# Token layers of a fused attention and mixer kernel: one pair of heads at a time, or two pairs in matmuls of 256 columns

## The chip, the cores and the metric

The kernel runs on one core of a Trainium2 chip. The metric is the device time of one execution in microseconds (us); lower is better. TensorE (PE in the profile) multiplies matrices into PSUM, VectorE (DVE) and ScalarE (ACT) read PSUM and write SBUF, GpSimd (POOL) works on SBUF, and SyncE (SP) issues most of the DMAs.

## The reference

```python
def reference(q, k, v, tau, w_tok1, w_tok2, w_ch1, w_ch2):   # q, k, v: (8, 12, 448, 64)
    q_n = q / (norm(q, axis=-1) + 1e-6)
    k_n = k / (norm(k, axis=-1) + 1e-6)
    attn = softmax(q_n @ k_n.transpose(0, 1, 3, 2) / tau)
    x = (attn @ v).transpose(0, 2, 1, 3).reshape(8, 448, 768)
    xt = x.transpose(0, 2, 1)
    h = relu(xt @ w_tok1) @ w_tok2          # token layers: 448 -> 256 -> 448
    u = x + h.transpose(0, 2, 1)
    return u + relu(u @ w_ch1) @ w_ch2      # channel layers: 768 -> 1536 -> 768
```

All inputs and the output are float32; the matmuls run in fp16 with float32 sums.

## The kernel before

The work is cut into 48 pairs of heads, six for each of the eight batches. A pair gives 128 of the 768 channels, so a pair's attention output `x` is 448 tokens by 128 channels, held as a tile of four windows of 128 tokens (tile `x`, 128 partitions, 4 x 128). The main loop has one turn for each pair from 7 to 47; here such a turn is called a segment and has its pair's number. An instruction stream is written out by hand in the order of the program, and each engine works its instructions in that order.

A segment `i` issues, in this order:

- three `score` calls for pair `i` (L345): matmuls of 64 rows into tiles `psS`, each followed by an exponential on ScalarE (L346);
- the value product of pair `i - 1`: `pv_rest` (L367, eight matmuls that alternate between the two tiles `psO_0` and `psO_1`) and `pv` (L384, 24 matmuls), then on VectorE a reciprocal (L387) and the scaling that writes `x` (L388). For the pairs below 12 there is no `pv_rest`, and the 32 matmuls of `pv` fill `psO_0` first and `psO_1` after it;
- `side(i)`: casts, squares and norms of later pairs on GpSimd and VectorE, loads and DMA transposes of later pairs on SP (`tpose_dma`, L330);
- one `unit(True)`, a piece of the channel layers of an earlier batch: `m_ch1` (tile `psG`, six matmuls of 448 columns, L467, and a ReLU on ScalarE, L470) or `m_ch2` (tile `psF`, twelve matmuls of up to 384 columns, L483, and one or two additions on VectorE, L487);
- `score_rest` (tile `psQ`, L352);
- `tok2(i - 2)`: the second token layer, eight matmuls of 128 columns into `psU` (L434), then the addition of `x` on VectorE (L437), which writes `u16`, then `udma`: a DMA transpose into `ut` on SP (L443). The channel layers read `ut`;
- below segment 13, `tpose(i + 1)`: transposes on TensorE into a tile `pst` (L322) and a copy on VectorE (L324);
- as many further units as are due by a budget in nanoseconds (`fed`, `due`): the first of them as `unit(True)`, all others as `unit()`;
- `tok1(i - 1)`: the first token layer, eight matmuls of 128 columns into `psR` (L420), then a ReLU on VectorE (L423) that writes `rt`;
- `sums(i + 3)`: a reduction on VectorE (L266).

PSUM has two pools, and a tile is given the slot that comes next in turn. What the order of the work means for a slot is that the first matmul of a tile waits until the reader of the slot's last tile has ended:

```python
    ps = ctx.enter_context(tc.tile_pool(name="ps", bufs=2, space=bass.MemoryType.PSUM))
    ps2 = ctx.enter_context(tc.tile_pool(name="ps2", bufs=3, space=bass.MemoryType.PSUM))
```

`psO_0`, `psO_1`, `psU`, `psR`, `pst` and the units called as `unit()` (here: narrow units) take the two slots of `ps` (tag `b`) in turn. `psS`, `psQ` and the units called as `unit(True)` (wide units) take the three slots of `ps2`.

After segment 47 a tail computes the channel layers of the last two batches with fewer products (`p1` to `p7`, L587; `q1` to `q7`, L675).

Of the kernel before, what the change touches and what calls it, by code (L numbers as in the profile page):

```python
# [7 lines left out]
FP32 = mybir.dt.float32  # L8
FP16 = mybir.dt.float16
AF = mybir.ActivationFunctionType  # L10
ALU = mybir.AluOpType
# [5 lines left out]
def _bcast_free(ap: bass.AP, n: int) -> bass.AP:  # L17
    new_ap = list(ap.ap) + [[0, n]]
    return bass.AP(tensor=ap.tensor, offset=ap.offset, ap=new_ap)
# [3 lines left out]
def kernel(  # L23
# [12 lines left out]
    nc = tc.nc  # L36

    B, H, S, E = q.shape
# [7 lines left out]
    TT = T // 128  # L46
    DH = 384
    NPAIR = H // 2
    NP_ALL = B * NPAIR
# [20 lines left out]
    def windows(b):  # L70
        return EVEN if b % 2 == 0 else ODD
# [11 lines left out]
    nrm = ctx.enter_context(tc.tile_pool(name="nrm", bufs=3))  # L83
# [6 lines left out]
    ps = ctx.enter_context(tc.tile_pool(name="ps", bufs=2, space=bass.MemoryType.PSUM))  # L90
    ps2 = ctx.enter_context(tc.tile_pool(name="ps2", bufs=3, space=bass.MemoryType.PSUM))

    half = {}
    pipe = {}
    ut = {}
    u16 = {}
    gts = {}

    def old(i):
        return i < OLD  # L100
# [58 lines left out]
    w1t = cst.tile([128, 5, T], FP16, name="w1t")  # L159
    w2n = outp.tile([128, TT, S], FP16, name="w2n", tag="ost")  # L160
    w2t = cst.tile([128, TT, S + 64], FP16, name="w2t")
# [192 lines left out]

    def pv_rest(i):
        if old(i):
            return
        st = pipe[i]  # L360
        st["x"] = nrm.tile([128, 4, 128], FP16, name=f"x_{i}", tag="x", bufs=3)
        st["psO"] = [ps.tile([128, 4, E + 2], FP32, name=f"psO_{i}_{hh}", tag="b") for hh in range(2)]
        for m, lo in enumerate(windows(i // NPAIR)):
            for hh in range(2):
                hb = slice(hh * 64, hh * 64 + 64)
                at = 2 * S * KC + lo
                nc.tensor.matmul(st["psO"][hh][:, m, 0:E + 1], pts[i % 2][hb, at:at + 128],  # L367
                                 vts[(i // HP) % NV][hb, i % HP, 2 * KC, 0:E + 1], start=(m == 0), stop=False)

    def pv(i, hh):  # L370
        st = pipe[i]
        vt = vts[(i // HP) % NV]
        if old(i):
            if hh == 0:
                st["x"] = nrm.tile([128, 4, 128], FP16, name=f"x_{i}", tag="x", bufs=3)
            n, nch = SC, NCH
            psO = ps.tile([128, 4, E + 2], FP32, name=f"psO_{i}_{hh}", tag="b")
        else:
            n, nch = 128, KC
            psO = st["psO"][hh]  # L380
        for m, lo in enumerate(windows(i // NPAIR)):
            for c in range(nch):
                at = (2 * c + hh) * S + lo
                nc.tensor.matmul(psO[:, m, 0:E + 1], pts[i % 2][0:n, at:at + 128], vt[0:n, i % HP, nch * hh + c, 0:E + 1],  # L384
                                 start=(old(i) and c == 0), stop=(c == nch - 1 and (old(i) or m == 3)))
        rec = nrm.tile([128, 4], FP32, name=f"rec_{i}_{hh}", tag="rec", bufs=4)
        nc.vector.reciprocal(out=rec[:], in_=psO[:, :, E])  # L387
        nc.vector.tensor_tensor(out=st["x"][:, :, hh * E:(hh + 1) * E], in0=psO[:, :, 0:E],  # L388
                                in1=_bcast_free(rec[:], E), op=ALU.mult)


    def pv_wide(i):
        st = pipe[i]
        vt = vts[(i // HP) % NV]
        st["x"] = nrm.tile([128, 4, 128], FP16, name=f"x_{i}", tag="x", bufs=3)
        psO = ps2.tile([128, 2, 512], FP32, name=f"psO_{i}", tag="s")
        o = psO[:, :, 0:4 * (E + 2)].rearrange("p h (m e) -> p h m e", m=4)
        for hh in range(2):
            for m, lo in enumerate(windows(i // NPAIR)):
                for c in range(NCH):  # L400
                    at = (2 * c + hh) * S + lo
                    nc.tensor.matmul(o[:, hh, m, 0:E + 1], pts[i % 2][0:SC, at:at + 128],
                                     vt[0:SC, i % HP, NCH * hh + c, 0:E + 1], start=(c == 0), stop=(c == NCH - 1))
        st["o"] = o

    def x_wide(i):
        st = pipe[i]
        o = st["o"]
        rec = nrm.tile([128, 2, 4], FP32, name=f"rec_{i}", tag="rec2", bufs=2)
        nc.vector.reciprocal(out=rec[:], in_=o[:, :, :, E])  # L410
        nc.vector.tensor_tensor(out=st["x"][:].rearrange("p m (h e) -> p h m e", h=2), in0=o[:, :, :, 0:E],
                                in1=_bcast_free(rec[:], E), op=ALU.mult)

    def tok1(i, wide=False):
        st = pipe[i]
        w1 = (0, 1, 2, 3) if (i // NPAIR) % 2 == 0 else (4, 0, 1, 2)
        psR = (ps2 if wide else ps).tile([128, TT, 128], FP32, name=f"psR_{i}", tag="s" if wide else "b")
        for tt in range(TT):
            for m in range(4):
                nc.tensor.matmul(psR[:, tt], w1t[:, w1[m], tt * 128:(tt + 1) * 128], st["x"][:, m],  # L420
                                 start=(m == 0), stop=(m == 3))
        st["rt"] = nrm.tile([128, TT, 128], FP16, name=f"rt_{i}", tag="rt", bufs=2)
        nc.vector.tensor_scalar_max(out=st["rt"][:], in0=psR[:], scalar1=0.0)  # L423

    def tok2(i, pe=False, wide=False):
        st = pipe[i]
        b, pj = i // NPAIR, i % NPAIR
        if pj == 0:
            u16[b] = mix.tile([128, DT, 4, 128], FP16, name=f"u16_{b}", tag="u16", bufs=4)
            ut[b] = mix.tile([128, DT, 4, 128], FP16, name=f"ut_{b}", tag="ut")  # L430
        psU = (ps2 if wide else ps).tile([128, 4, 128], FP32, name=f"psU_{i}", tag="s" if wide else "b")
        for m, lo in enumerate(windows(b)):
            for tt in range(TT):
                nc.tensor.matmul(psU[:, m], w2t[:, tt, lo:lo + 128], st["rt"][:, tt],  # L434
                                 start=(tt == 0), stop=(tt == TT - 1))
        u = u16[b][:, pj]
        nc.vector.tensor_tensor(out=u, in0=psU[:], in1=st["x"][:], op=ALU.add)  # L437
        if not pe:
            udma(i)

    def udma(i):
        b, pj = i // NPAIR, i % NPAIR
        nc.sync.dma_start_transpose(out=ut[b][:, pj], in_=u16[b][:, pj].rearrange("p m d -> p (m d)"))  # L443
# [132 lines left out]
    e = {}  # L576
# [195 lines left out]
    with tc.manual_schedule():  # L772
# [3 lines left out]
            name=nc.get_next_instruction_name(), act_func_set_id=ACT_SET_LN_EXP,  # L776
# [94 lines left out]
        i = NPAIR  # L871
# [48 lines left out]
        for i in range(NPAIR + 1, NP_ALL):  # L920
            b, pj = i // NPAIR, i % NPAIR
            for c in range(KC):
                score(i, c)
                if c == 1 and NP_ALL - 6 <= i < NP_ALL - 2:
                    norms(i + 2)
            if i == NPAIR + 1:
                upose(i - 4, 2)
                tok2(i - 2, pe=True)
                pv_wide(i - 1)
                upose_act(i - 2)  # L930
                x_wide(i - 1)
                sums(i + 2)
            else:
                pv_rest(i - 1)
                pv(i - 1, 0)
                pv(i - 1, 1)
            if i == NP_ALL - 1:
                fast_weights1(2, nc.vector)
            if i == NPAIR + 1:
                refill(0)  # L940
            elif pj == 2 and 1 < b < B - 1:
                refill(b - 1)
            side(i)
            if i == NP_ALL - NPAIR:
                fed[1] = (sum(t for t, _ in queue) - fed[0]) / NPAIR
            fed[0] += fed[1]
            unit(True)
            if old(i):
                score(i, KC)
            else:  # L950
                score_rest(i)
            if i > NPAIR + 1:
                tok2(i - 2)
            if i + 1 < DMA_T0:
                tpose(i + 1)
            if due():
                unit(True)
            while due():
                unit()
            tok1(i - 1)  # L960
            if i + 3 < NP_ALL:
                sums(i + 3)
            if i == NP_ALL - 3:
                early.close()
                tail = ctx.enter_context(tc.tile_pool(name="tail", bufs=1, side="right", reuse_waits="tile"))
                tail_tiles()
            if i == NP_ALL - 2:
                fast_weights2(2, (1,))
                fast_weights1(1, nc.gpsimd)
            if i == NP_ALL - 1:  # L970
                fast_weights1(4, nc.gpsimd)
# [139 lines left out]
```

## Time and profile before

| | us |
|---|---|
| median of 3 runs | 383.1 (382.84 to 383.28) |
| the profiled execution | 380.6 |
| its span, from the first to the last instruction | 378.8 |
| TensorE busy | 366.2 |
| GpSimd, VectorE, ScalarE busy | 286.9, 246.0, 234.0 |
| `psR` matmuls (L420) busy | 29.3 |
| `psU` matmuls (L434) busy | 29.3 |

The profile is that of one execution, 2.5 us below the median of the runs. A matmul's record lasts longer than the time in which the next one can follow it, because matmuls are pipelined: the distance from one start to the next is read off the timeline, where `x8` stands for eight records merged into one line. Segment 13 begins at 79.02 us, segment 47 at 316.93 us, and a segment between them lasts from 4.7 to 8.4 us, according to the units that it holds.

### The profile page before, as it was taken

The numbers are of one execution on the slowest core, as the hardware profiler recorded it, in microseconds if no ns is written. First come the engines' busy times: TensorE is split into PE (matmuls) and PEld (weight loads), VectorE is DVE, ScalarE is ACT, GpSimd is POOL, SyncE is SP. The second block draws the span as 40 slices with busy tenths as digits, with TensorE's granted clock in tenths as the row PEclk, the third lists the DMA queues.
The fourth block names the chain that finished last, engine by engine and source line by source line (L and its number), as shares of the span: only waits on it lengthen the run. The fifth ranks groups of instructions, "written<-read, shape, count | busy, mean of one in ns | idle before, by whom it ended". The sixth has DMA issues, their size and how long they took to land.

```text
span 378.8 us, 10270 instructions
## 1 busy us (share of the span) xinstructions
PE 366.2 (97%) x4086; PEld 240.1 (63%) x4086; DVE 246.0 (65%) x559; ACT 234.0 (62%) x401; POOL 286.9 (76%) x414
## 2 busy tenths in 40 slices
PE   7788999999999999999999999999999999999994
PEld 6466666676567666667656666666666667655562
DVE  7789766777436574557444675456545776887963
ACT  5999887855666447855675466764677574426410
POOL 8999997979667577678657757767869987389760
PEclk9999999999999999999999999999999999999999
DMA  8999999989997898969895798977984874200144
GB/s 225 281 231 218 262 239 200 207 159 157 217 220 141 180 201 209 187 167 170 213 210 121 175 184 198 195 162 197 205 192 104 158 160 99 57 0 3 55 123 116
DMA packets 116256, 64.35 MB, mean 170 GB/s; under 512 B 72304, under 2 KB 112880, under 8 KB 116208
## 3 DMA queue, kind: packets, MB, share of 16 engines
q1 hardware_dynamic: 110208, 58.20, 69.9%
q0 software_dynamic: 5616, 5.21, 8.7%
q8 instruction: 32, 0.52, 0.6%
q10 hardware_dynamic: 384, 0.29, 0.2%
q14 instruction: 16, 0.13, 0.1%
HBM read 43.45 MB, written 11.01 MB: 144 GB/s over the span
## 4 chain that ended last, share of the span: by engine, by line
PE 81%; DMA 7%; DVE 4%; POOL 3%; ACT 1%; issue 1%; SPq 0%; DVEq 0%; POOLq 0%
PE psG L467 21%; PE psF L483 19%; PE psO L384 9%; PE psS L345 7%; PE psU L434 5%; PE psR L420 5%; DMA qf<-in_q_dram 3%; PE psY L587 3%; PE psYo L675 2%; DMA kf<-in_k_dram 2%; PE psX L587 2%; PE psQ L352 2%; POOL kq L298 2%; PE psZ L587 2%; PE psZo L675 1%; DVE ssq L266 1%
## 5 line engine op out<-in xcount | busy, mean ns | idle before, releaser
L346 ACT ACTIVATE pt<-psS 128x896 f16<-128x896 f32 (+1 forms) x156 | 132.7, 916 | 51.9 <-PE psS L345 51.9
L483 PE MATMUL psF<-wc2t,gt 128*128 128x384 f16 x504 | 88.4, 326 | 0.0
L467 PE MATMUL psG<-ut,wc1t 128*128 128x448 f16 x432 | 88.1, 352 | 0.0
L298 POOL TENSOR_TENSOR kq<-kf,rn 128x384 f16<-128x384 f32 (+1 forms) x47 | 41.9, 891 | 59.2 <-DVE rn L275 55.6
L483 PEld LDWEIGHTS <-gt 128*128 128x128 f16 x504 | 47.1, 98 | 27.8
L467 PEld LDWEIGHTS <-wc1t 128*128 128x128 f16 x432 | 40.2, 98 | 32.4
L470 ACT ACTIVATE gt<-psG 128x448 f16<-128x448 f32 x72 | 38.9, 540 | 33.1 <-PE psG L467 33.1
L266 DVE TENSOR_REDUCE ssq<-sq 128x15 f32<-128x960 f32 (+2 forms) x51 | 56.2, 1101 | 2.9 <-ACT sq L248 1.8
L423 DVE TENSOR_SCALAR rt<-psR 128x256 f16<-128x256 f32 x48 | 20.1, 418 | 50.8 <-PE psR L420 50.8
L298 POOL TENSOR_TENSOR kq<-qf,rn 112x512 f16<-112x512 f32 x45 | 47.0, 1045 | 3.0
L345 PE MATMUL psS<-qk 64*128 64x448 f16 x312 | 41.3, 355 | 3.5 <-DVE qk L324 2.8
L487 DVE TENSOR_TENSOR ost<-psF,u 128x384 f32<-128x384 f32 (+1 forms) x48 | 25.7, 536 | 26.8 <-PE psF L483 25.4
L250 POOL TENSOR_TENSOR sq<-qf 112x512 f32<-112x512 f32 x39 | 40.6, 1040 | 0.0
L250 POOL TENSOR_TENSOR sq<-kf 128x384 f32<-128x384 f32 (+1 forms) x46 | 40.2, 873 | 0.3 <-DMA kf<-in_k_dram 0.3
L384 PE MATMUL psO<-vt,pt 128*128 128x65 f16 (+1 forms) x1024 | 39.2, 193 | 0.0
L388 DVE TENSOR_TENSOR x<-psO,rec 128x256 f16<-128x256 f32 x82 | 34.8, 425 | 2.8
L384 PEld LDWEIGHTS <-pt 128*128 128x128 f16 (+1 forms) x1024 | 34.2, 97 | 3.5 <-issue 0.9
L437 DVE TENSOR_TENSOR u<-psU,x 128x512 f16<-128x512 f32 x48 | 32.3, 674 | 2.0 <-PE psU L434 0.5
L434 PEld LDWEIGHTS <-w2t 128*128 128x128 f16 x384 | 24.8, 98 | 7.9 <-issue 1.0
L420 PEld LDWEIGHTS <-w1t 128*128 128x128 f16 x384 | 24.8, 98 | 7.9 <-issue 2.1
L434 PE MATMUL psU<-rt,w2t 128*128 128x128 f16 x384 | 29.3, 219 | 0.5 <-POOL w2t L198 0.5
L420 PE MATMUL psR<-x,w1t 128*128 128x128 f16 x384 | 29.3, 219 | 0.2 <-DVE u L437 0.2
(128 smaller groups left out, 481.0 us busy)
## 6 DMA issues: line engine op xcount, KB each, us to landing
qf<-in_q_dram SPq DMA_DIRECT2D x47, 224.0 KB, 4.2
kf<-in_k_dram SPq DMA_DIRECT2D x36, 192.0 KB, 3.9
vf<-in_v_dram SPq DMA_DIRECT2D x36, 192.0 KB, 3.8
vf<-in_v_dram SPq DMA_DIRECT2D x12, 224.0 KB, 7.6
kf<-in_k_dram SPq DMA_DIRECT2D x11, 224.0 KB, 7.2
wc1t<-in_moe_w_ch_dram POOLq DMA_DIRECT2D x4, 576.0 KB, 10.1
wc2t<-in_moe_w_ch_dram POOLq DMA_DIRECT2D x2, 1152.0 KB, 11.8
out_dram<-ost SPq DMA_DIRECT2D x6, 336.0 KB, 3.6
```

The source lines that it names most:

```text
L250: nc.gpsimd.tensor_mul(out=dst, in0=src, in1=src)
L266: nc.vector.tensor_reduce(out=st["ssq"][0:n, sl], in_=st["sq"][0:n, sl], axis=AXX.X, op=ALU.add)
L298: eng.tensor_tensor(out=kq[0:p, a, 0:n].rearrange("p c g e -> p g c e"), in0=st["kq"[a]][:].rearrange("p (g c) e -> p g c e", g=2), in1=_b ...
L345: nc.tensor.matmul(psS[:, hh, 0:S], qk[hb, c * n:c * n + 128], qm[hb], start=True, stop=True)
L346: nc.scalar.activation(out=pts[i % 2][0:n, 2 * S * c:2 * S * (c + 1)].rearrange("p (h s) -> p h s", h=2), in_=psS[0:n, :, 0:S], func=AF.Ex ...
L384: nc.tensor.matmul(psO[:, m, 0:E + 1], pts[i % 2][0:n, at:at + 128], vt[0:n, i % HP, nch * hh + c, 0:E + 1], start=(old(i) and c == 0), st ...
L388: nc.vector.tensor_tensor(out=st["x"][:, :, hh * E:(hh + 1) * E], in0=psO[:, :, 0:E], in1=_bcast_free(rec[:], E), op=ALU.mult)
L420: nc.tensor.matmul(psR[:, tt], w1t[:, w1[m], tt * 128:(tt + 1) * 128], st["x"][:, m], start=(m == 0), stop=(m == 3))
L434: nc.tensor.matmul(psU[:, m], w2t[:, tt, lo:lo + 128], st["rt"][:, tt], start=(tt == 0), stop=(tt == TT - 1))
L467: nc.tensor.matmul(psG[:, 0:S], wc1t[:, dt, ct * 128:(ct + 1) * 128], ut[b][:, dt].rearrange("p m s -> p (m s)")[:, lo:lo + S], start=(dt ...
L470: nc.scalar.activation(out=gt[:, ct, (b % 2) * S:(b % 2 + 1) * S], in_=psG[:, 0:S], func=AF.Relu)
L483: nc.tensor.matmul(psF[:, 0:hi - lo], gt[:, ct, at:at + 128], wc2t[:, ct, lo:hi], start=(ct == 0), stop=(ct == CT - 1))
```

## The change

From the second batch on, the token layers of two neighbouring pairs (an even one and the odd one after it) are computed together. A tile `xx` holds the `x` of both pairs, and `x_tile(i)` gives a pair its half of it. `tok1(i - 2, 2)` runs in even segments only and computes the first token layer of the pairs `i - 2` and `i - 1` with eight matmuls of 256 columns into one tile `psR`, followed by one ReLU of 512 elements in each partition. `tok2(i - 3, 2)` runs in odd segments only and computes the second layer of the pairs `i - 3` and `i - 2` in two tiles `psU`, each with four matmuls of 256 columns and one addition of 512 elements, and then issues the two DMA transposes. The weights are loaded once for both pairs. The first batch and the last two pairs, 46 and 47, stay one by one. `rt` has one buffer in place of two, of twice the size; `xx` has two in place of the three of `x`.

```diff
+    def x_tile(i):
+        if i % 2 == 0:
+            pipe[i]["xx"] = nrm.tile([128, 4, 2, 128], FP16, name=f"x_{i}", tag="x", bufs=2)
+        pipe[i]["x"] = pipe[i - i % 2]["xx"][:, :, i % 2]
+
     def pv_rest(i):
...
-        st["x"] = nrm.tile([128, 4, 128], FP16, name=f"x_{i}", tag="x", bufs=3)
+        x_tile(i)
...
-    def tok1(i, wide=False):
-        st = pipe[i]
+    def tok1(i, n=1):
         w1 = (0, 1, 2, 3) if (i // NPAIR) % 2 == 0 else (4, 0, 1, 2)
-        psR = (ps2 if wide else ps).tile([128, TT, 128], FP32, name=f"psR_{i}", tag="s" if wide else "b")
+        j = slice(i % 2, i % 2 + n)
+        psR = ps.tile([128, TT, n, 128], FP32, name=f"psR_{i}", tag="b")
         for tt in range(TT):
             for m in range(4):
-                nc.tensor.matmul(psR[:, tt], w1t[:, w1[m], tt * 128:(tt + 1) * 128], st["x"][:, m],
+                nc.tensor.matmul(psR[:, tt], w1t[:, w1[m], tt * 128:(tt + 1) * 128], pipe[i - i % 2]["xx"][:, m, j],
                                  start=(m == 0), stop=(m == 3))
-        st["rt"] = nrm.tile([128, TT, 128], FP16, name=f"rt_{i}", tag="rt", bufs=2)
-        nc.vector.tensor_scalar_max(out=st["rt"][:], in0=psR[:], scalar1=0.0)
-
-    def tok2(i, pe=False, wide=False):
-        st = pipe[i]
+        pipe[i]["rt"] = rt = nrm.tile([128, TT, n, 128], FP16, name=f"rt_{i}", tag="rt", bufs=1)
+        nc.vector.tensor_scalar_max(out=rt[:], in0=psR[:], scalar1=0.0)
+
+    def tok2(i, n=1, pe=False):
         b, pj = i // NPAIR, i % NPAIR
...
-        psU = (ps2 if wide else ps).tile([128, 4, 128], FP32, name=f"psU_{i}", tag="s" if wide else "b")
-        for m, lo in enumerate(windows(b)):
-            for tt in range(TT):
-                nc.tensor.matmul(psU[:, m], w2t[:, tt, lo:lo + 128], st["rt"][:, tt],
-                                 start=(tt == 0), stop=(tt == TT - 1))
-        u = u16[b][:, pj]
-        nc.vector.tensor_tensor(out=u, in0=psU[:], in1=st["x"][:], op=ALU.add)
+        x, rt = pipe[i - i % 2]["xx"], pipe[i]["rt"]
+        for k in range(n):
+            at = range(4 // n * k, 4 // n * (k + 1))
+            psU = ps.tile([128, 4 // n, n, 128], FP32, name=f"psU_{i}_{k}", tag="b")
+            for m in at:
+                lo = windows(b)[m]
+                for tt in range(TT):
+                    nc.tensor.matmul(psU[:, m - at[0]], w2t[:, tt, lo:lo + 128], rt[:, tt],
+                                     start=(tt == 0), stop=(tt == TT - 1))
+            nc.vector.tensor_tensor(out=u16[b][:, pj:pj + n, at[0]:at[-1] + 1].rearrange("p j m d -> p m j d"),
+                                    in0=psU[:], in1=x[:, at[0]:at[-1] + 1, i % 2:i % 2 + n], op=ALU.add)
         if not pe:
-            udma(i)
+            for j in range(n):
+                udma(i + j)
...
-            if i > NPAIR + 1:
-                tok2(i - 2)
+            if i > NPAIR + 1 and i % 2:
+                tok2(i - 3, 2)
...
-            tok1(i - 1)
+            if i % 2 == 0:
+                tok1(i - 2, 2)
+            elif i == NP_ALL - 1:
+                tok1(i - 1)
```

More of the change, by code (lines that the diff above doesn't have):

```diff
@@ L374, in pv @@
             if hh == 0:
-                st["x"] = nrm.tile([128, 4, 128], FP16, name=f"x_{i}", tag="x", bufs=3)
+                x_tile(i)
             n, nch = SC, NCH
@@ L394, in pv_wide @@
         vt = vts[(i // HP) % NV]
-        st["x"] = nrm.tile([128, 4, 128], FP16, name=f"x_{i}", tag="x", bufs=3)
+        x_tile(i)
         psO = ps2.tile([128, 2, 512], FP32, name=f"psO_{i}", tag="s")
@@ L410, in x_wide @@
         nc.vector.reciprocal(out=rec[:], in_=o[:, :, :, E])
-        nc.vector.tensor_tensor(out=st["x"][:].rearrange("p m (h e) -> p h m e", h=2), in0=o[:, :, :, 0:E],
+        nc.vector.tensor_tensor(out=st["x"].rearrange("p m (h e) -> p h m e", h=2), in0=o[:, :, :, 0:E],
                                 in1=_bcast_free(rec[:], E), op=ALU.mult)
-    def tok1(i, wide=False):
-        st = pipe[i]
+    def tok1(i, n=1):
         w1 = (0, 1, 2, 3) if (i // NPAIR) % 2 == 0 else (4, 0, 1, 2)
-        psR = (ps2 if wide else ps).tile([128, TT, 128], FP32, name=f"psR_{i}", tag="s" if wide else "b")
+        j = slice(i % 2, i % 2 + n)
+        psR = ps.tile([128, TT, n, 128], FP32, name=f"psR_{i}", tag="b")
         for tt in range(TT):
             for m in range(4):
-                nc.tensor.matmul(psR[:, tt], w1t[:, w1[m], tt * 128:(tt + 1) * 128], st["x"][:, m],
+                nc.tensor.matmul(psR[:, tt], w1t[:, w1[m], tt * 128:(tt + 1) * 128], pipe[i - i % 2]["xx"][:, m, j],
                                  start=(m == 0), stop=(m == 3))
-        st["rt"] = nrm.tile([128, TT, 128], FP16, name=f"rt_{i}", tag="rt", bufs=2)
-        nc.vector.tensor_scalar_max(out=st["rt"][:], in0=psR[:], scalar1=0.0)
-    def tok2(i, pe=False, wide=False):
-        st = pipe[i]
+        pipe[i]["rt"] = rt = nrm.tile([128, TT, n, 128], FP16, name=f"rt_{i}", tag="rt", bufs=1)
+        nc.vector.tensor_scalar_max(out=rt[:], in0=psR[:], scalar1=0.0)
+    def tok2(i, n=1, pe=False):
         b, pj = i // NPAIR, i % NPAIR
```

## The prediction

> **What bounds the kernel.** I read the page first (busy shares, chain of waits, groups), then busy time by stretch, then the timeline of TensorE and VectorE around the token layers.
>
> ```profile
> PE 366.2 (97%) x4086; PEld 240.1 (63%) x4086; DVE 246.0 (65%) x559; ACT 234.0 (62%) x401; POOL 286.9 (76%) x414
> PE 81%; DMA 7%; DVE 4%; POOL 3%; ACT 1%; issue 1%; SPq 0%; DVEq 0%; POOLq 0%
> ```
>
> ```profile
> 79.00:289.00 210.00, 210.00 (x2341) 137.29 (x2339) 120.30 (x298) 130.81 (x234) 150.49 (x245) 1.00 0.85 183
> ```
>
> TensorE has no gap from 79 to 289 us (210.00 of 210.00, full clock), and the chain is its matmuls. There every nanosecond given to or taken from TensorE's stream counts; other engines count only where TensorE waits for them. From 289 to 310 us the chain passes through POOL and a DMA transpose, but segment 46's first score waits only some 0.25 us for it.
>
> Next, the end of segment 23, with a narrow `psG` before `psR`:
>
> ```profile
> 157.12 0.61 PE L420 MATMUL psR<-x,w1t 128*128 128x128 f16 x8
> 157.32 0.54 ACT L470 ACTIVATE gt<-psG 128x448 f16<-128x448 f32 x1 [0.59 <-PE psG L467]
> 157.67 0.74 PE L345 MATMUL psS<-qk 64*128 64x448 f16 x6
> 157.77 0.43 DVE L423 TENSOR_SCALAR rt<-psR 128x256 f16<-128x256 f32 x1 [2.95 <-PE psR L420]
> 158.24 0.28 PE L367 MATMUL psO<-vt,pt 64*128 64x65 f16 x8
> 158.46 0.92 PE L384 MATMUL psO<-vt,pt 128*128 128x65 f16 x24
> ```
>
> The new `psO_1` takes `psR`'s slot, so its first matmul, second of the eight, needs the ReLU's end: 158.20, against 158.24. The cover is used up. Where the ReLU came later, behind an addition (end of segment 13), one sees the price:
>
> ```profile
> 83.38 0.69 DVE L437 TENSOR_TENSOR u<-psU,x 128x512 f16<-128x512 f32 x1
> 83.99 0.41 DVE L423 TENSOR_SCALAR rt<-psR 128x256 f16<-128x256 f32 x1
> ```
>
> ```profile
> 83.72 0.74 PE L345 MATMUL psS<-qk 64*128 64x448 f16 x6
> 84.30 0.43 PE L367 MATMUL psO<-vt,pt 64*128 64x65 f16 x8
> 84.66 0.93 PE L384 MATMUL psO<-vt,pt 128*128 128x65 f16 x24
> ```
>
> The eight take 0.36 instead of 0.23 (91.08 to 91.31, where segment 15 begins and nothing is late), so 0.13 is lost; the ReLU ended at 84.40, 0.10 after their start. Loss = ReLU's end minus start of the eight, plus 0.04. The cases at 294.36 and 305.84 give the same.
>
> **The change, part by part.**
>
> *Matmuls.* Rates from starts: 128 columns 55.6 ns (`psU` 153.27, next 153.72: 0.445 for 8), 384 columns 162.4, 448 columns 189: columns/2.4 + 2.4 ns. 256 columns, between those rows, come to 109. Pairs 6 to 45 are 20 doubles: 16 matmuls of 109 replace 32 of 55.6, or 320 x (111.2 - 109) = **-0.8 us**. The weight loads saved were already hidden: a pair of load and matmul passes in those 55.6 ns.
>
> The Trainium skill ("TensorE: Matmul & The Clock Gate", Back-to-back issue gap) puts a sustained load-and-matmul stream at 81 ns for 128 columns and 131 for 512; interpolated to 98 for 256, an estimate, it would save 320 x 64 ns = 20 us. The rows here say 55.6, and I follow them.
>
> *The ReLU of a double set.* No row has this form; it lies between its own half (0.42) and the 512-element addition (0.69). The scaling of `x` grows from 0.42 to 0.69 from 256 to 512 elements, so I add 0.27: 0.68. From `psR`'s first start T: eight matmuls 0.87; ReLU starts 0.21 later as before (157.12 + 0.445 to 157.77), at T+1.08, ends T+1.76. The eight of `psO` start 0.675 after `psR` as before (0.1 change to 64-row matmuls, 0.575 `psS`), at T+1.55. Loss 0.21 + 0.04 = 0.25 at each even segment's end, from 12 to 46: 18 x 0.25 = 4.5, less 0.27 already lost at 42 and 44: **+4.2** (0 with a ReLU of 0.42; 4.4 with 0.69). Segments 8 and 10 are free: those pairs fill `psO_0` first.
>
> The Trainium skill ("Perfetto Trace Analysis", Optimizing Scalar/DVE Operations) advises breaking up VectorE instructions that leave bubbles on another engine; this goes the other way. Two ReLUs of 256 would end at about T+1.5, with no loss by the formula.
>
> *Odd segments' ends.* No `psR` now lies between the last narrow unit and `psS`, so that unit's reader meets `psO_1`. It ends 0.74 (ScalarE, above) to 0.76 (VectorE's addition) after the unit; `psO` comes at 0.675: loss 0.105 to 0.125. Segments 15, 17, 19, 21, 23, 27, 29, 31, 33, 35, 39, 41 end so: **+1.3** (0 if the reader ends sooner; the 0.14 seen above at most, 1.7). 25, 37, 43 end in a wide unit: nothing. 13 and 45 have no unit after `psU`, and the second addition ends some 0.4 and 0.17 after `psO` is due: 0.44 - 0.13 and 0.21, **+0.5**.
>
> *Transposes.* In segments 9 and 11, two `psU` tiles fill both slots, so `pst` waits for the first addition, which VectorE starts only after the norms (57.21 to 57.90; `pst` would be due at 56.55 + 0.87 = 57.42): 0.52 each, **+1.0** (0 to 1.4, two additions).
>
> *Segment 47.*
>
> ```profile
> 320.69 1.14 DVE L487 TENSOR_TENSOR ost<-psF,u 64x384 f32<-64x384 f32 x2
> 321.86 0.69 DVE L437 TENSOR_TENSOR u<-psU,x 128x512 f16<-128x512 f32 x1
> ```
>
> The single `psR` of pair 46 now gets the first `psU`'s slot: free at 322.55, due at 320.63 + 0.87 = 321.50. 1.09 lost, less 0.16 that `psO` waited there before: **+0.9**.
>
> *The rest.* Segment 7 loses `psR` (0.45 of work that moves into later sets) but its scores still wait for the copy of `qk` (ends 46.06): +0.15. The 0.25 us wait at segment 46 absorbs as much: -0.25. VectorE saves 20 x 0.15 on ReLUs, off the path. SP's two `u` transposes (1.2 us each to issue) go back to back every second segment; behind them stand output stores and the next `qk` transpose, issued at 157.04 and needed at 164.61, so 1.2 later costs nothing. Batches' last pairs are transposed in the same segment as before. `rt`'s single buffer is read out by TensorE before the next `psR`.
>
> Sum: -0.8 + 4.2 + 1.3 + 0.5 + 1.0 + 0.9 + 0.15 - 0.25 = **+7.0**. On the profiled 380.6 (378.8 span and 1.8 around it) that is 387.6; the median of the runs is 2.5 higher, so 390.1.
>
> **The rivals.**
>
> *The slots are free in time (faster).* If readers of PSUM end before the slot is wanted, only the matmul term stays: 382.3. It decides where the doubled ReLU lasts under 0.43 (then T+1.51 is early enough) and the other readers shrink likewise. For: before, 158.20 was just in time. Against: VectorE's own rows grow by 0.27 with 256 elements. 0.07.
>
> *Only the ReLU's wait counts.* Narrow units, `pst` and segment 47 hide theirs: 383.1 - 0.8 + 4.2 = 386.5. For: 0.1 us effects lie at the limit of what I can read from merged rows. 0.15.
>
> *SP becomes late.* From segment 42 on, `qk` transposes land just when wanted (306.41 plus 3.84, and TensorE waited). If the second `u` transpose stands in front of them in three segments, 3 x 1.2 = 3.6 more: 393.7. Against: segment 44's, the critical one, has no `u` transpose of its own segment before it. 0.08.
>
> **How the numbers follow.** The forecast has 0.70. The range goes from 385.6 (the forecast without the ReLU's term is 385.9, and it holds the second case) to 392.5 (the terms at their upper ends add 1.0: ReLU 0.2, narrow units 0.4, transposes 0.4; 1.4 more are for waits not seen); it leaves out the first and the last case. Within 0.2% (0.8 us) is about what a measurement can't tell from no change: 0.02. Faster by more than that: 0.07, the first case as far as it reaches beyond. Slower: 0.91.
>
> **What would show it.** Right: `psR` and `psU` sets of eight in 0.87 us; a ReLU of some 0.68; after even segments 0.47 instead of 0.22 us between the starts of L367's and L384's successors, after odd ones 0.33; TensorE waiting for VectorE at `pst` twice. Wrong: eight matmuls of 256 in clearly less than 0.85 us, a ReLU under 0.45, or `psO` sets unchanged; then the time falls below the one before.

## The result, and the profile after

The changed kernel takes 391.3 us (median of 6 runs, 390.5 to 392.4); the kernel before takes 382.2 (6 runs, 380.3 to 383.3; its first three runs had the median 383.1). The ratio is 1.025 (1.021 to 1.028): the change makes the kernel 9.2 us slower. The forecast was 390.1 us, from +7.0 us on a before of 383.1. The profiled execution of the changed kernel took 391.5, with a span of 389.6.

The page of the changed kernel, busy shares and chain of waits:

```profile
PE 371.9 (95%) x3766; PEld 231.4 (59%) x3766; DVE 248.7 (64%) x539; ACT 232.9 (60%) x401; POOL 287.4 (74%) x414
...
PE 80%; DVE 11%; ACT 6%; issue 1%; DMA 1%; DVEq 0%; ACTq 0%
...
L428 DVE TENSOR_SCALAR rt<-psR 128x512 f16<-128x512 f32 (+1 forms) x28 | 17.1, 611 | 31.0 <-PE psR L425 30.9
```

TensorE issues 320 matmuls fewer, and yet the span is 10.7 us longer (378.83 to 389.55 before rounding). Its share of the chain hardly moves. The other shares have to be read by stretch: ScalarE's 6% lies wholly ahead of segment 13, in the start-up. From the start of segment 13 to that of segment 47 the chain has only TensorE, 0.6% of issue and three readers of PSUM on VectorE: the ReLU that writes `rt` (4.9%), the addition that writes `u` (1.1%) and the one that writes `ost` (0.7%). TensorE now waits, many times and briefly, for such readers. The ReLU of a double set is in the last line, mixed with the short ones of single pairs.

The timeline of the changed kernel shows how (start, duration, engine, line). Here are an even segment without `psU` (22, from its `psQ` on) and all of segment 23:

```profile
148.08 2.53 ACT L346 ACTIVATE pt<-psS 128x896 f16<-128x896 f32 x3
...
150.34 0.35 PE L352 MATMUL psQ<-qk 128*128 128x448 f16 x1
...
150.66 3.56 PE L476 MATMUL psG<-ut,wc1t 128*128 128x448 f16 x18
...
154.07 1.04 PE L425 MATMUL psR<-x,w1t 128*128 128x256 f16 x8
...
155.14 0.69 DVE L428 TENSOR_SCALAR rt<-psR 128x512 f16<-128x512 f32 x1 [3.59 <-PE psR L425]
...
155.61 0.55 PE L372 MATMUL psO<-vt,pt 64*128 64x65 f16 x8
...
156.09 0.92 PE L389 MATMUL psO<-vt,pt 128*128 128x65 f16 x24
...
158.18 1.04 PE L442 MATMUL psU<-rt,w2t 128*128 128x256 f16 x8
...
159.05 3.57 PE L476 MATMUL psG<-ut,wc1t 128*128 128x448 f16 x18
...
162.66 0.54 ACT L479 ACTIVATE gt<-psG 128x448 f16<-128x448 f32 x1 [0.59 <-PE psG L476]
...
163.13 0.40 PE L372 MATMUL psO<-vt,pt 64*128 64x65 f16 x8
163.46 0.92 PE L389 MATMUL psO<-vt,pt 128*128 128x65 f16 x24
```

Read from start to start. The set of `psU` takes 159.05 - 158.18 = 0.87. The double ReLU runs from 155.14 to 155.83; the eight matmuls of `psO` begin at 155.61 and take 0.48 to 156.09, where the kernel before took 0.22 at the same place (150.97 to 151.19, below). In the next segment, behind a narrow unit, they take 0.33 (163.13 to 163.46), and ScalarE's read of that unit ends at 163.20. These are the two waits that the forecast rests on. A third is new: `psG` follows `psQ` after 0.32 (150.34 to 150.66) instead of the 0.19 after which `psU` followed in the kernel before, and the exponentials that read the `psS` tiles end at 148.08 + 2.53 = 150.61.

A fourth shows where the segment before ended in a wide unit. The changed kernel at the start of segment 26, then the kernel before at the start of segment 23 and of segment 26:

```profile
176.61 0.55 PE L345 MATMUL psS<-qk 64*128 64x448 f16 x4
176.71 0.56 DVE L496 TENSOR_TENSOR ost<-psF,u 128x384 f32<-128x384 f32 x1 [1.10 <-PE psF L492]
...
177.32 0.36 PE L345 MATMUL psS<-qk 64*128 64x448 f16 x2 [0.17 <-DVE ost L496]
```

```profile
150.97 0.28 PE L367 MATMUL psO<-vt,pt 64*128 64x65 f16 x8
151.19 0.93 PE L384 MATMUL psO<-vt,pt 128*128 128x65 f16 x24
...
171.27 0.74 PE L345 MATMUL psS<-qk 64*128 64x448 f16 x6
171.85 0.30 PE L367 MATMUL psO<-vt,pt 64*128 64x65 f16 x8
```

Before, the six score matmuls run through in one group, and the eight follow 0.58 after its start. After, the third `psS` waits for the reader of the wide `psF`: VectorE's addition ends at 177.27, the matmul starts at 177.32, and four matmuls at 0.097 would have put it at 177.00. That is 0.32 lost.

In time, the 10.7 us of span fall into three parts by the starts of segments. Segment 7 begins 1.04 later (39.62 to 40.66). The segments 7 to 46 together grow by 8.70. Segment 47 and the tail grow by 0.98. The first part is no effect of the change: over the ten profiles of this study segment 7 begins anywhere from 39.62 to 41.91, in the order of the clock that TensorE was granted in the start-up. Between 10.5 and 20 us that clock is 1.00 in the four profiles that begin segment 7 at 39.62 to 40.23, two of which (wait filled, ReLU in two pieces) hold both double layers; it is 0.82 in the four at 40.26 to 40.84, the changed kernel's among them, and 0.64 in the two at 41.66 and 41.91. From 20 us to segment 47 it is 1.00 before and after, so the growth there is not a slower clock. By segment, odd ones from 15 to 41 grow by 0.22 to 0.25, and even ones from 16 to 44 by about 0.1, 0.23 or 0.31, by which of the waits above they hold.

### The profile page after: what moved, and what is told of

Its sections match the earlier page's. It is cut to its first block, busy times and chain, and to the rows that moved or that the text cites. A ratio compares the mean times of both kernels' runs of the same rounds, so it can differ in the third digit from the quotient of the medians.

```text
span 389.6 us, 9591 instructions
## 1 busy us (share of the span) xinstructions
PE 371.9 (95%) x3766; PEld 231.4 (59%) x3766; DVE 248.7 (64%) x539; ACT 232.9 (60%) x401; POOL 287.4 (74%) x414
## 4 chain that ended last, share of the span: by engine, by line
PE 80%; DVE 11%; ACT 6%; issue 1%; DMA 1%; DVEq 0%; ACTq 0%
PE psF L492 21%; PE psG L476 20%; PE psO L389 9%; PE psR L425 5%; PE psU L442 4%; ACT pt L346 4%; PE psS L345 4%; DVE rt L428 3%; PE psY L596 3%; PE psYo L684 2%; PE psO L372 2%; DVE ssq L266 2%; PE psX L596 2%; PE psQ L352 2%; PE psZ L596 1%; DVE u L444 1%
## 5 line engine op out<-in xcount | busy, mean ns | idle before, releaser
L345 PE MATMUL psS<-qk 64*128 64x448 f16 x312 | 42.4, 356 | 4.6 <-DVE qk L324 3.3
L496 DVE TENSOR_TENSOR ost<-psF,u 128x384 f32<-128x384 f32 (+1 forms) x48 | 26.6, 555 | 30.7 <-PE psF L492 29.1
L428 DVE TENSOR_SCALAR rt<-psR 128x512 f16<-128x512 f32 (+1 forms) x28 | 17.1, 611 | 31.0 <-PE psR L425 30.9
L393 DVE TENSOR_TENSOR x<-psO,rec 128x256 f16<-128x256 f32 x82 | 34.8, 424 | 2.8
L392 DVE RECIPROCAL rec<-psO 128x4 f32<-128x4 f32 x82 | 14.3, 174 | 31.3 <-PE psO L389 31.3
L444 DVE TENSOR_TENSOR u<-psU,x 128x512 f16<-128x512 f32 x48 | 31.1, 683 | 1.0
L353 ACT ACTIVATE pt<-psQ 128x448 f16<-128x448 f32 x36 | 19.5, 541 | 19.1 <-PE psQ L352 19.1
L345 PEld LDWEIGHTS <-qk 64*128 64x128 f16 x312 | 11.9, 94 | 26.0 <-issue 15.2
L425 PE MATMUL psR<-x,w1t 128*128 128x256 f16 (+1 forms) x224 | 25.7, 257 | 1.1 <-DVE u L444 1.1
```

The lines of the kernel that those rows point to most:

```text
L345: nc.tensor.matmul(psS[:, hh, 0:S], qk[hb, c * n:c * n + 128], qm[hb], start=True, stop=True)
L444: nc.vector.tensor_tensor(out=u16[b][:, pj:pj + n, at[0]:at[-1] + 1].rearrange("p j m d -> p m j d"), in0=psU[:], in1=x[:, at[0]:at[-1] + ...
```

## The experiments

Gaps are to the median of the 17 runs of before that were made with an experiment; each experiment has 5 or 6 runs, two have 12. The changed kernel was not run again beside them, so a difference against it is a difference of two gaps. The theory: the time is lost at slots of PSUM whose readers end too late, by the formula of the prediction (the reader's end, less the start that was due, plus 0.04), most of it to the ReLU of 512 elements. The rivals: the wider matmuls themselves cost something; the fewer buffers do; SP is late.

**Half of the ReLU.**

```diff
...
+        if n == 2:
+            pipe[i]["rt"] = rt = rt2
+            nc.vector.tensor_scalar_max(out=rt[:, :, 0], in0=psR[:, :, 0], scalar1=0.0)
+            return
```

> The changed kernel, but the ReLU of a double set works on 256 of its 512 elements in each partition (the other half is left out). Slot theory: the ReLU lasts 0.42 us instead of 0.69 and ends before psO_1 is due, so the eight matmuls of pv_rest take 0.23 us again after even segments: 18 x 0.25 = 4.5 us less than the changed kernel, some 4.7 us above the kernel before. Rival (the matmuls of 256 columns or the moved work cost the time, the ReLU is hidden): no change against the changed kernel.

Measured: 387.4 (386.0 to 388.8), ratio 1.012 (1.008 to 1.016). The gap to before is 4.8 instead of 9.2: 4.4 us less. TensorE's timeline of this kernel, after an even segment:

```profile
111.83 0.28 PE L374 MATMUL psO<-vt,pt 64*128 64x65 f16 x8
112.04 0.92 PE L391 MATMUL psO<-vt,pt 128*128 128x65 f16 x24
```

The eight are back at 0.21 to 0.22 at all 18 places; after odd segments they keep 0.33. All other parts of the change are in place, so the length of this one VectorE instruction is worth some 4.4 us (18 x 0.26 are 4.7). Of a faster TensorE, segment 44 gives a little back: there its scores wait 1.2 us for the DMA transpose of `qk`, which they do not in the changed kernel:

```profile
307.97 0.74 PE L347 MATMUL psS<-qk 64*128 64x448 f16 x6 [1.21 <-DMA qk<-kq]
```

**Filling the wait.** The first `score` of odd segments computes its two matmuls twice, ahead of the eight.

```diff
+        if c == 0 and i % 2 and i > OLD:
+            for hh in range(2):
+                hb = slice(hh * 64, hh * 64 + 64)
+                nc.tensor.matmul(psS[:, hh, 0:S], qk[hb, c * n:c * n + 128], qm[hb], start=True, stop=True)
```

> The changed kernel, and in odd segments from 13 on the two matmuls of the first score tile run twice: 0.19 us more of work in front of pv_rest, 18 times, 3.4 us in sum (the second run writes the same values again). Slot theory: it lies inside the 0.25 us that psO_1 waits for the ReLU, so the eight matmuls of pv_rest shrink from 0.48 to 0.29 us and the time stays that of the changed kernel. Rival (no wait is there, TensorE only works more slowly around the new sets): 3.4 us more.

Measured: 391.2 (390.5 to 392.9), ratio 1.023 (1.019 to 1.026), a gap of 8.7. TensorE's timeline of this kernel:

```profile
109.13 1.04 PE L429 MATMUL psR<-x,w1t 128*128 128x256 f16 x8
110.10 0.36 PE L345 MATMUL psS<-qk 64*128 64x448 f16 x2
110.30 0.35 PE L349 MATMUL psS<-qk 64*128 64x448 f16 x2
110.49 0.54 PE L345 MATMUL psS<-qk 64*128 64x448 f16 x4
110.87 0.36 PE L376 MATMUL psO<-vt,pt 64*128 64x65 f16 x8
111.16 0.92 PE L393 MATMUL psO<-vt,pt 128*128 128x65 f16 x24
```

The extra pair takes 0.19 (110.30 to 110.49), and the eight shrink from 0.48 to 0.29: from `psR` to L393 it is 2.03, as in the changed kernel (154.07 to 156.09: 2.02). TensorE was idle there, and the wait is for an end that is fixed by VectorE, not a slower rate of the matmuls.

**Two shorter ReLUs.** A double `psR` is two tiles, one for each half of the 256 hidden channels, each with its own ReLU.

```diff
...
+        for t0 in range(n):
+            t1 = t0 + 1 if n == 2 else TT
+            psR = ps.tile([128, t1 - t0, n, 128], FP32, name=f"psR_{i}_{t0}", tag="b")
...
+            nc.vector.tensor_scalar_max(out=rt[:, t0:t1], in0=psR[:], scalar1=0.0)
```

> The changed kernel, but the first layer of two pairs goes into two tiles psR_0 and psR_1 of 256 elements in each partition, each with its own ReLU. Slot theory: the second ReLU ends 1.50 us after the set's start, before psO_1 is due at 1.55, so the 0.25 us after even segments go; in the seven segments that end in a narrow psG, psR_1 instead waits 0.34 us for that unit's ReLU, as its slot is the unit's. 11 x 0.25 less, 7 x 0.09 more: 2.1 us below the changed kernel. Rival (more VectorE instructions cost more): above the changed kernel.

Measured: 389.5 (389.0 to 390.8), ratio 1.020 (1.017 to 1.022), a gap of 7.4: 1.8 less than the changed kernel's, with intervals that overlap, and 2.1 were expected. TensorE's timeline of this kernel:

```profile
108.92 0.60 PE L428 MATMUL psR<-x,w1t 128*128 128x256 f16 x4
109.72 0.60 PE L428 MATMUL psR<-x,w1t 128*128 128x256 f16 x4 [0.19 <-ACT gt L481]
...
110.82 0.28 PE L372 MATMUL psO<-vt,pt 64*128 64x65 f16 x8
111.04 0.92 PE L389 MATMUL psO<-vt,pt 128*128 128x65 f16 x24
```

The loss at `psO` is gone (0.22). But `psR` now takes both slots, and the second half takes that of the last narrow unit: it starts at 109.72 instead of 108.92 + 0.44, and the loss has moved ahead. By the starts of segments, which vary less than the medians, odd segments from 13 to 41 are 0.26 to 0.28 shorter than in the changed kernel, and the seven that end in a narrow `psG` (16, 22, 24, 28, 34, 36, 40) are 0.35 to 0.38 longer. The Trainium skill ("Perfetto Trace Analysis", Optimizing Scalar/DVE Operations) says that breaking up VectorE instructions that cause bubbles on another engine may let work finish sooner; it holds here for the bubble itself, and for less than half of it in the time, because each piece needs a slot.

**`psR` early.** In even segments the double `tok1` stands right behind `score_rest`, ahead of the units, and the unit behind it is a narrow one.

```diff
+            if i > OLD and i % 2 == 0:
+                tok1(i - 2, 2)
...
-                unit(True)
+                unit(i <= OLD or i % 2 == 1)
...
-            if i % 2 == 0:
+            if i <= OLD and i % 2 == 0:
```

> The changed kernel, but in even segments from 14 on tok1 of the two pairs stands directly behind score_rest (where tok2 stands in odd segments), and the units due after it are all narrow. Slot theory: a unit now lies between psR and the next segment, so the ReLU's wait of 0.25 us becomes that of a narrow unit, 0.11, in 15 segments (2.1 us less), and psR covers the 0.13 us that a wide psG behind psQ waits for the third exponential in 7 segments (0.9 less): some 3 us below the changed kernel, 5.7 above the kernel before. Rival (the place of the sets does not matter, their form does): no change against the changed kernel.

Measured: 388.4 (387.4 to 389.4), ratio 1.017 (1.014 to 1.019), a gap of 6.2: 2.9 less. TensorE's timeline of this kernel:

```profile
105.57 0.35 PE L352 MATMUL psQ<-qk 128*128 128x448 f16 x1
105.76 1.04 PE L425 MATMUL psR<-x,w1t 128*128 128x256 f16 x8
106.63 4.70 PE L476 MATMUL psG<-ut,wc1t 128*128 128x448 f16 x24
...
111.84 0.40 PE L372 MATMUL psO<-vt,pt 64*128 64x65 f16 x8
112.17 0.92 PE L389 MATMUL psO<-vt,pt 128*128 128x65 f16 x24
```

The ReLU has 5 us before its slot is wanted. In its place the last narrow unit's reader meets `psO`, so 0.33 remains of the 0.48, and `psG` no longer follows `psQ` at all. The eight fall to 0.33 to 0.35 at 15 places (at the starts of 13, 43 and 45 they stay at 0.48): 15 x 0.14, and 7 x 0.13 for the gap behind `psQ`, are 3.0 against the measured 2.9. What remains is the wait that odd segments have anyway: with `psR` gone from the end of a segment, some reader is always too late.

**The matmuls one by one.** As the changed kernel, but each set of eight with 256 columns is sixteen with 128, weights loaded for each.

```diff
+            for g in range(n):
+                for m in range(4):
+                    nc.tensor.matmul(psR[:, tt, g], w1t[:, w1[m], tt * 128:(tt + 1) * 128],
+                                     pipe[i - i % 2]["xx"][:, m, i % 2 + g], start=(m == 0), stop=(m == 3))
...
+                for g in range(n):
+                    for tt in range(TT):
+                        nc.tensor.matmul(psU[:, m - at[0], g], w2t[:, tt, lo:lo + 128], rt[:, tt, g],
+                                         start=(tt == 0), stop=(tt == TT - 1))
```

> The changed kernel with its order, tiles, ReLUs, additions and transposes, but each matmul of 256 columns is two of 128, each with its own weight load. Theory: the wider matmuls are worth 320 x 2.2 ns = 0.7 us, so this is 0.7 us above the changed kernel, and sets of sixteen take 0.89 us. Rival (weight loads cost time in a stream of loads and matmuls, 81 ns for 128 columns against 98 for 256): 20 us above the changed kernel.

Measured: 392.2 (391.4 to 392.7), ratio 1.026 (1.023 to 1.029), a gap of 10.0: 0.9 more than the changed kernel's, with intervals that overlap. A set of `psU`, from its start to that of the next unit, in this kernel:

```profile
113.43 1.06 PE L444 MATMUL psU<-rt,w2t 128*128 128x128 f16 x16
114.32 3.57 PE L478 MATMUL psG<-ut,wc1t 128*128 128x448 f16 x18
```

The sixteen take 0.89 where the eight wide ones take 0.87, and from segment 13 to 42 every segment lasts 0.01 to 0.03 longer than in the changed kernel. Over 40 sets that is some 0.8 us, which the medians alone can't tell from nothing. The 20 us estimated from the Trainium skill's figures ("TensorE: Matmul & The Clock Gate", Back-to-back issue gap) are excluded.

**Buffers alone.** The order of the kernel before, with the new tiles (`xx` twice, `rt` once).

```diff
-            if i > NPAIR + 1 and i % 2:
-                tok2(i - 3, 2)
+            if i > NPAIR + 1:
+                tok2(i - 2)
...
-            if i % 2 == 0:
-                tok1(i - 2, 2)
...
+            tok1(i - 1)
```

> The tiles of the change (xx for two pairs with two buffers, rt with one buffer, psU as in the change) with the matmuls and the order of before: one pair at a time in both layers. Theory: nothing waits for these buffers, so the time is that of the kernel before (within 0.3 us), and the start of segment 7, 1.0 us later in the changed kernel's profile, moves by chance from run to run. Rival (the buffers cost the first 40 us their 1.0): 1 us above the kernel before.

Measured: 381.9 (380.8 to 383.4, 12 runs), ratio 0.999 (0.997 to 1.002). The buffers cost nothing: from segment 13 to 44 every segment lasts as long as before, within 0.01 us. Its profiled segment 7 begins at 40.63, as late as the changed kernel's, at the same granted clock of 0.82 between 10.5 and 20 us, and the runs show no loss of time against before: the 1.04 us of the start are not the change's.

**The second layer alone.** `tok1` runs in each segment and its ReLU writes half of a shared `rt`; `tok2` is double.

```diff
...
+        nc.vector.tensor_scalar_max(out=rt[:, :, k:k + 1], in0=psR[:], scalar1=0.0)
...
-            if i % 2 == 0:
-                tok1(i - 2, 2)
...
+            tok1(i - 1)
```

> Only the second token layer is doubled (in odd segments), the first runs for one pair at the end of every segment. Slot theory: with psR back at every segment's end, neither the ReLU's wait nor the waits after odd segments are there; left are the transposes (1.0), the unit behind psQ in even segments (0.9), segments 13 and 45 (0.7) and 47 (0.9), less 0.35 for the matmuls: some 3.2 us above the kernel before, 6 below the changed kernel. Rival (both layers cost alike): 4.6 above before.

Measured: 384.6 (383.4 to 388.6, 12 runs), ratio 1.006 (1.003 to 1.009), a gap of 2.0 (1.2 to 3.3 by the ratio's interval). From segment 7 on its profile is 3.0 longer than that of before, close to the 3.2 expected. TensorE's timeline of this kernel:

```profile
103.77 0.35 PE L352 MATMUL psQ<-qk 128*128 128x448 f16 x1
104.08 4.70 PE L480 MATMUL psG<-ut,wc1t 128*128 128x448 f16 x24
...
109.74 0.28 PE L372 MATMUL psO<-vt,pt 64*128 64x65 f16 x8
109.95 0.92 PE L389 MATMUL psO<-vt,pt 128*128 128x65 f16 x24
```

With `psR` in each segment's end again, the eight take 0.21 to 0.24 everywhere. The gap behind `psQ` is there (0.31): it comes with `psU` leaving even segments, not with `tok1`. So some 2 to 3 us of the 9.2 belong to the second layer, and by difference the rest to the first.

**The first layer alone: a miss.** `tok1` is double, `tok2` runs pair by pair; for that the odd pair's `tok2` had to come one segment later.

```diff
...
-            if i > NPAIR + 1 and i % 2:
-                tok2(i - 3, 2)
+            if i > NPAIR + 2:
+                tok2(i - 3)
+            if i == NP_ALL - 1:
+                tok2(i - 2)
```

> Only the first token layer is doubled (in even segments), the second runs for one pair in every segment. Slot theory: the ReLU's wait stays whole (4.5 us), and so do the waits after odd segments (12 narrow units x 0.11, five wide units x 0.3: 2.8); the waits at the transposes (1.0) and of the unit behind psQ in even segments (7 x 0.13 = 0.9) go. Some 1.5 us less than the changed kernel, 7.7 above the kernel before. Rival (both layers cost alike): halfway, 4.6 above before.

Measured: 408.8 (408.3 to 410.7), ratio 1.069 (1.065 to 1.073), a gap of 26. TensorE's waits in this kernel (us in total, times, longest), then SP's and TensorE's timelines of the first place, and busy time of the engines in the last stretch of it (after the busy times, the granted clock):

```profile
PE psG L478 <- DMA ut<-u: 12.4, 5, 3.8
```

```profile
91.72 1.23 SPq L330 DMA_TRANSPOSE qk<-kq  x1
...
97.70 1.27 SPq L454 DMA_TRANSPOSE ut<-u  x1
```

```profile
100.60 5.01 PE L478 MATMUL psG<-ut,wc1t 128*128 128x448 f16 x13 [3.58 <-DMA ut<-u]
```

```profile
100.60:105.54 4.94, 4.94 (x14) 1.73 (x14) 0.00 (x0) 1.09 (x2) 0.06 (x1) 0.50 0.91 215
```

The last pair of the second batch is added at 88.78 to 89.47. Its transpose is issued at 97.70, eight microseconds later, because SP has a `qk` transpose that waits for GpSimd, loads and output stores ahead of it. `psG` of that batch is next on TensorE and stands until 100.60. In the kernel before the last pair was added a segment sooner in the order, its transpose was issued at 88.97, and `psG` began at 94.66 without a wait. The 12.4 us are the greater part of the 17 us by which this kernel is slower than the changed one. The rest comes with them: around the three longest of the five waits (3.6, 3.8 and 2.5 us) the granted clock is 0.50, from 99.8 to 106.6, 198.8 to 202.2 and 294.3 to 297.7 us, and matmuls of 448 columns follow each other after 373 ns instead of 189. Half of these 13.6 us, 6.8, is an estimate of what that cost; with the 12.4 it more than covers the 17 us.

The total therefore says little of the first layer, but the segments without such a wait do. Two neighbouring segments, in us:

| | segments 17 and 18 | segments 23 and 24 |
|---|---|---|
| before | 13.90 | 14.22 |
| both layers double | 14.24 | 14.69 |
| first layer alone | 14.26 | 14.58 |
| second layer alone | 13.88 | 14.32 |

The first layer alone adds 0.36 to each, the second -0.02 and 0.10, and together they come to what the change adds, 0.34 and 0.47. So the larger part of the loss is seen at the first layer itself, and not only as a difference. The run also shows that the changed kernel depends on doing the last pair of a batch, an odd one, in the same segment as before.

## Why the prediction was right, and where not

*Right in mechanism, and in most sizes.* The matmuls: sets of eight in 0.87, as worked out, and -0.8 us agrees with the run with single matmuls (its own factors, 320 x 2.2 ns, give 0.7). The ReLU: 0.69 (taken: 0.68), 0.48 instead of 0.22 at the eight, at 18 places, and 4.4 us by the run with half of it (taken: 4.2). Odd segments' ends: 0.33 to 0.35 instead of 0.22 to 0.23, 0.11 to 0.12 a piece (taken: 0.105 to 0.125). The transposes and segment 47, from TensorE's timelines of the changed kernel:

```profile
57.57 1.05 PE L442 MATMUL psU<-rt,w2t 128*128 128x256 f16 x8
58.96 0.56 PE L322 MATMUL pst<-id,kq 112*128 112x112 f16 x8 [0.35 <-DVE u L444]
```

```profile
320.21 0.19 PE L372 MATMUL psO<-vt,pt 64*128 64x65 f16 x1
320.64 0.28 PE L372 MATMUL psO<-vt,pt 64*128 64x65 f16 x7 [0.24 <-DVE u L444]
320.85 0.93 PE L389 MATMUL psO<-vt,pt 128*128 128x65 f16 x24
...
330.63 1.04 PE L442 MATMUL psU<-rt,w2t 128*128 128x256 f16 x8
332.60 0.61 PE L425 MATMUL psR<-x,w1t 128*128 128x128 f16 x8 [0.94 <-DVE u L444]
```

From `psU` to `pst` it is 1.39, that is 0.52 over the 0.87 of the matmuls: exactly the term. From `psU` to `psR` in segment 47 it is 1.97, or 1.10 too long, as the 1.09 of the prediction. The quarter that segment 46's wait was to absorb is there too: segment 45 becomes 0.10 shorter, although it begins with the 0.25 of a double ReLU.

*The step that failed: "25, 37, 43 end in a wide unit: nothing".* I followed the wide unit's reader to `psO`, whose slots are in the other pool, and stopped. But the third `psS` of the next segment takes the wide unit's own slot. Before, `psR` stood between them; now it meets the reader, at 0.3 each. The same happens behind segments 9 and 11, where the sum had only the transposes. Five places, 1.5 us.

*A term that was missing: `psG` behind `psQ`.* In seven even segments (16, 22, 24, 28, 34, 36, 40) a wide `psG` follows `psQ` directly, since `psU` has moved to the odd segment, and takes the third `psS`'s slot before its exponential has ended: 0.13 each, 0.9 us. `psU` had hidden that with its 0.445. In its wording the prediction asked of each slot what became late when a set was moved in; it did not ask what had been hidden by the set that was moved out.

*A term too small:* segment 45's end, taken at 0.21; the rows at 320.21 show 0.64 for the eight, 0.42 lost. At segment 13's end 0.44 was about right (0.42).

With these three, 7.0 + 1.5 + 0.9 + 0.2 = 9.6. The profile shows 8.70 + 0.98 = 9.7 from segment 7 on, the medians show 9.2. Of the small terms, segment 7's +0.15 did not come (it became 0.04 shorter). So the sum missed some 2.2 us of the measured 9.2, a quarter. The forecast time came within 1.2 us by luck, because the 383.1 it was put on was 1 us above the later median of before.

*The rivals.* Slots free in time: excluded by the 0.48. Only the ReLU's wait counts: excluded by the `pst`, `psR` and L372 rows; the run with half the ReLU still is 4.8 us slower than before. SP late: not in the changed kernel, whose waits name no DMA at a score; but SP is near it, since the half-ReLU run waits for its transposes 1.2 us at a score, and the first-layer run 12.4 us at `psG`.

No variant with wide sets beats the kernel before. At most 0.8 us could be had from the wide matmuls, if every wait found cover, and the best variant with both layers in wide sets that leaves no work out (`psR` early) is still 6.2 us slower than before.

## What to carry to other kernels

When TensorE has no gap, small sets of matmuls between others are also the time in which the readers of PSUM finish. Before they are merged, list for each slot the reader that must end while the set runs, both where the merged set goes and where the old one is taken away, and in each pool; compare the reader's end with the next tile's start. A merged set has a longer reader too, and here that alone cost five times what the matmuls could save.

## What the runs showed of the hardware

- A stream of matmuls that loads weights each time is as fast by the column with 128 columns as with 256: sixteen of 128 take 0.89 (0.87 for eight of 256), and the 320 loads and matmuls saved were worth 0.9 us, within the intervals.
- Waits of 0.1 to 0.3 us at a slot mostly don't appear as TensorE's waits. They are in the view of the weight loader's waits, without a releaser (total, times, longest), here of the changed kernel:

```profile
PEld L345 <- issue: 15.2, 51, 0.4
PEld L372 <- issue: 10.5, 33, 0.5
```

  Before, the line of the eight (L367) had 1.1 us in 4 such waits, and the changed kernel has 33. The distances from start to start on the timeline are what gives them a size.
- In ten profiles with nearly the same first instructions segment 7 starts between 39.62 and 41.91 us, the later the longer TensorE was granted half its clock in the start-up (0, 3.4 or 6.8 us between 11 and 19 us). So a comparison of two spans should begin behind the start-up.
- In the run of the first layer alone, the clock was also halved for 3.4 to 6.8 us around the three waits of 2.5 to 3.8 us; around its two shorter waits, 0.9 and 1.6 us, it stayed at 1.00.
